# Routing of a fused attention and mixture-of-experts kernel in pieces: batches of 11, 9 and 4 units, four early and six late weight units

## The chip, the cores and the metric

The kernel runs on 1 core of one Trainium2 chip. The metric is the device time of one execution in microseconds (us). The kernel before takes 732.75 us, the median of 3 runs (731.21 to 734.17). Besides these there is one profiled execution, from which all rows below come.

## What is computed

Three layers run one after the other on 3072 tokens of 384 values. Cut to what matters, the reference is:

```python
# 1: gated linear attention, 4 batches x 8 heads x 768 steps, head size 48
state = alpha[t][:, None] * state + outer(k[t], v[t])
x[t] = q[t] @ state
# 2: a router, and 8 experts
do_compute = x @ w_skip > 0
xc = x[do_compute]
e_idx = argmax(xc @ w_gate)
gate_w = softmax(xc @ w_gate)[e_idx]
x[do_compute] = xc + gate_w * (relu(xc @ w1[e_idx]) @ w2[e_idx])   # 384 -> 1024 -> 384
# 3: a dense layer over all tokens
h = x @ w_in                                                       # 384 -> 2048
out = (h - tanh(h)) @ w_out                                        # 2048 -> 384
```

About half of the tokens skip the experts. The weights of the dense layer are float64.

## The kernel before

**Stages.** The order of the instructions on each engine is the order in which the program text issues them. Four stages follow each other.

1. *The attention loop.* `astep(s)` runs for s = 0 to 23. A unit is 128 tokens of one batch entry with all 8 heads, and there are 24. Step s works on several units at once. SP issues the loads `aload(s+4)` (`it`: alpha, q, k) and `vload(s+3)` (`vt`). VectorE runs the two scans of unit s+2 (`F` and `G`, L196 and L203), then the mask of unit s (`am`, L234). GpSimd makes `qh`, `kh` and `pf` of unit s+2 (L209, L214, L221). TensorE makes `pa` of unit s (L229), then `py` of unit s-1 (L243, L250), then `px` of unit s-2 (L297: the token rows and the router's logits), and the state (`pd`, L274, L277). `pa` has one PSUM buffer, so TensorE's `pa` of unit s+1 waits for the mask of unit s. Steps 20 to 23 have no state to update and are shorter.
2. *Fill.* The first `NE0` of the 16 weight units of the dense layer are split into a high and a low part in the attention loop ("early" units, `wsplit`). Row block 0 of the dense layer (512 tokens that skip the experts) is multiplied by these units (`mm1b`, L465, and `mm2b`, L499) while the last routing, the scatters and the first expert weights are under way.
3. *Experts.* 64 weight units, 8 to an expert (`mm1`, L561, and `mm2`, L579 to L581).
4. *Dense layer.* 6 row blocks of 512 tokens by 16 weight units. Block 0 lacks the units that the fill did. The last `NLATE` weight units are split here ("late" units), one every two steps.

**Routing.** Tokens are routed in three batches of units, `BATCHES = (12, 8, 4)`. `route1` (L328 to L352: logits `lg`, maximum `mx`, differences `dl`, the one-hot choice `oa`) and `route1b` (L360 to L369) run on VectorE. `route2` (L376, L378) ranks the tokens of the batch by matmuls of `oa` into `pr` on TensorE, `evr` (L385) copies the ranks to SBUF on ScalarE, and `route3` (L393 to L412) turns them into row numbers `loc` on VectorE. Then `scatter(u)` (L416) writes the 128 rows of unit u to the buffer `xb` in DRAM by an indirect DMA that GpSimd issues. For batch 0, `route1` and `route1b` stand behind the mask in step 13, `route2` at the end of step 13, `evr` and `route3` in step 14; for batch 1 the same in steps 21 and 22. Batch 2 comes behind the loop.

**Around it.** `rload(0)` (L430) reads the 512 rows of block 0 from `xb` on SP in step 21, after all scatters of batch 0. `split2(0, a)` transposes them (L438, TensorE) and splits them in steps 22 and 23. `xload` (L540) reads an expert's rows `xe` from `xb`, and the first two wait for all 24 scatters. The `xb` rows of the experts are first filled from `zero` in steps 6 to 9 (L687). An early weight unit is loaded by `wload` (768 KB, L125) and split in pieces `s0` to `s3`: `s0` (L155, L156), `s1` (L160 and two ScalarE copies), `s2` (L166, L167), `s3` (L170).

The step functions that set the order:

```python
    for k in range(NE0):
        at[max(1, 4 * k)].append(lambda k=k: wload(NMU + k))
        early = wsplit(NMU + k)
        for s, f_ in zip((3, 4, 4, 6), early):
            if k < NE0 - 1:
                aft[4 * k + s].append(f_)
    for i in range(BATCHES[0]):
        aft[14 + 7 * i // BATCHES[0]].append(lambda i=i: scatter(i))
```

`at[s]` runs at the start of step s, and `aft[s]` behind its mask.

Of the kernel before, what the change touches and what calls it, by code (L numbers as in the profile page):

```python
# [21 lines left out]
NU = B * NC_  # L22
# [17 lines left out]
RING = 8  # L40
LA = RING - 3
RAWS = 5
NE0 = 5
NLATE = 5

# [5 lines left out]
TOP = NS + N - 1  # L53
NROWS = NS + N
NCL = NE + 2
BATCHES = (12, 8, 4)
NB = max(BATCHES)
XW = PD + 9

# [2 lines left out]
def tile_kernel(ctx: ExitStack, tc: tile.TileContext, att0, att, vt, wsg, wmoe, wff, out):  # L62
# [56 lines left out]
    def wload(i):  # L119
        if i < NMU or not wide:  # L120
            raw_t[i] = rings["raw"].tile([128, W], F32, tag="raw", name=f"raw{i}")
            nc.sync.dma_start(raw_t[i], wmoe[i] if i < NMU else wff[i - NMU])
        else:
            raw_t[i] = cvp.tile([128, W, 2], U32, tag="raw64", name=f"raw{i}")
            nc.sync.dma_start(raw_t[i].rearrange("p a b -> p (a b)"), wff[i - NMU].bitcast(U32))  # L125

    def wsplit(i):

        own = (ring if i % RING < RING0 else rings["ring2"]) if i < NMU else ffE if i < NMU + NE0 else None
        late = i >= NMU + NF2 - NLATE  # L130
        t_ = {}

        def alloc():
            src = own or rings["late" if late else "R"]
            t_["h"] = src.tile([128, W], F32R, tag="wh", name=f"wh{i}")
            t_["l"] = src.tile([128, W], F32R, tag="wl", name=f"wl{i}")
            w_t[i] = (t_["h"], t_["l"])

        def n0():
            alloc()  # L140
            A.copy(t_["h"], raw_t[i])  # L141

        def n1():
            V.tensor_tensor(t_["l"], raw_t[i], t_["h"].bitcast(F32), ALU.subtract)  # L144

        if i < NMU or not wide:
            return [n0, n1]


        def s0():  # L150
            up = raw_t[i][:, :, 1]
            t_["s"] = cvp.tile([128, W], U32, tag="cs", name=f"cs{i}")
            t_["a"] = cvp.tile([128, W], U32, tag="ca", name=f"ca{i}")
            t_["f"] = cvp.tile([128, W], F32, tag="cl", name=f"cl{i}")
            V.tensor_scalar(t_["s"], up, 3, 0x3FFFFFFF, ALU.logical_shift_left, ALU.bitwise_and)  # L155
            V.scalar_tensor_tensor(t_["a"], up, 0xC0000000, t_["s"], ALU.bitwise_and, ALU.bitwise_or)  # L156

        def s1():
            A.activation(t_["f"], raw_t[i][:, :, 0], AF.Copy, scale=2.0 ** -52)
            V.tensor_scalar(t_["s"], t_["a"], 0xFF800000, None, ALU.bitwise_and)  # L160
            alloc()
            A.copy(t_["h"], t_["a"].bitcast(F32))

        def s2():
            a_ = t_["a"].bitcast(F32)
            V.tensor_tensor(t_["f"], t_["f"], t_["s"].bitcast(F32), ALU.mult)  # L166
            V.tensor_tensor(a_, a_, t_["h"].bitcast(F32), ALU.subtract)  # L167

        def s3():
            V.tensor_tensor(t_["l"], t_["a"].bitcast(F32), t_["f"], ALU.add)  # L170

        return [s0, s1, s2, s3]


    U = [dict() for _ in range(NU)]
# [137 lines left out]
    def t3(n, c, k=NE, dt=F32):  # L313
        return rt.tile([128, NB, k], dt, tag=n, name=f"{n}{c}", bufs=1)[:, :BATCHES[c]]

# [9 lines left out]
    def route1(c):  # L325
        r = RT[c]
        lg = t3("lg", c, 9)
        V.tensor_reduce(lg, r["l4"].rearrange("p b a k -> p b k a"), axis=AX.X, op=ALU.add)  # L328
        mx = t1("mx", c)
        V.tensor_reduce(mx, lg[:, :, 1:9], axis=AX.X, op=ALU.max)  # L330
        dl = t3("dl", c)
        V.tensor_tensor(dl, lg[:, :, 1:9], bc(mx), ALU.subtract)
        r["ex"] = t3("ex", c)
        A.activation(r["ex"], dl, AF.Exp)

        cand = t3("cand", c)
        V.tensor_scalar(cand, dl, 0.0, None, ALU.is_equal)
        V.tensor_tensor(cand, cand, bb(em99, c), ALU.mult)
        fi = t1("fi", c)
        V.tensor_reduce(fi, cand, axis=AX.X, op=ALU.min)  # L340
        V.tensor_scalar(fi, fi, 99.0, None, ALU.add)
        oh = t3("oh", c)
        V.tensor_tensor(oh, bb(eidx, c), bc(fi), ALU.is_equal)

        oa = rt.tile([128, NB + 1, NCL], BF16, tag="oa", name=f"oa{c}", bufs=1)[:, :BATCHES[c] + 1]
        V.memset(oa[:, BATCHES[c]], 0.0)
        r["oaz"], oa = oa, oa[:, :BATCHES[c]]
        ac = t1("ac", c)
        V.tensor_scalar(ac, lg[:, :, 0], 0.0, None, ALU.is_gt)
        V.tensor_tensor(oa[:, :, :NE], oh, bc(ac), ALU.mult)  # L350
        V.tensor_scalar(oa[:, :, NE], ac, -1.0, 1.0, ALU.mult, ALU.add)
        V.tensor_copy(oa[:, :, NE + 1], ac)  # L352
        r["oa"], r["ac"], r["fi"] = oa, ac, fi

    def route1b(c):

# [24 lines left out]
    def evr(c):  # L381
        r = RT[c]
        n = BATCHES[c]
        t_ = rt.tile([128, NB + 1, NCL], F32, tag="prs", name=f"prs{c}", bufs=1)[:, :n + 1]
        A.copy(flat(t_), r["pr"])  # L385
        r["prv"], r["prt"] = t_[:, :n], t_[:, n]
# [27 lines left out]
    def scatter(u):  # L414
        k, i = where[u]
        s_ = nc.gpsimd.indirect_dma_start(  # L416
            xb[:, :], bass.IndirectOffsetOnAxis(loc[:, u:u + 1], 0), RT[k]["xr"][:, i, :], None,
            bounds_check=NROWS - 1, oob_is_err=False)
        if u:
            tc.declare_no_dep(s_.ins, group="route", reason="rows of their own")  # L420
        tc.add_to_no_dep_group("route", s_.ins)
# [263 lines left out]
    for s in range(6, 6 + NS // 512):  # L685
        r0 = 512 * (s - 6)
        at[s].append(lambda r0=r0: nc.sync.dma_start(  # L687
            xb[r0:r0 + 512, :].rearrange("(a p) d -> p a d", a=4), zero.unsqueeze(1).to_broadcast([128, 4, RW])))
    for k in range(NE0):
        at[max(1, 4 * k)].append(lambda k=k: wload(NMU + k))  # L690
        early = wsplit(NMU + k)
        for s, f_ in zip((3, 4, 4, 6), early):
            if k < NE0 - 1:
                aft[4 * k + s].append(f_)
    at[21].append(lambda: rload(0))
    for i in range(BATCHES[0]):
        aft[14 + 7 * i // BATCHES[0]].append(lambda i=i: scatter(i))

    def astep(s):

        def ok(u):
            return 0 <= u < NU

        def pX_(name):
            return ps["T"].tile([128, 512], F32, tag="X", name=name)

        if ok(s + 4):
            aload(s + 4)
        if ok(s + 3):
            vload(s + 3)  # L710
        for f_ in at[s]:
            f_()
        mmA(s)
        if ok(s - 2):
            evx(s - 2)
        c1 = next((k for k in range(len(BATCHES)) if s == first[k] + BATCHES[k] + 1), None)
        c3 = next((k for k in range(len(BATCHES)) if s == first[k] + BATCHES[k] + 2), None)
        if c3 is not None:
            evr(c3)
        if ok(s + 2):  # L720
            scanF(s + 2)
            mkqh(s + 2)
            scanG(s + 2)
            mkkh(s + 2)
            mkpf(s + 2)
        if ok(s - 1):
            mmYs(s - 1)
        trk(s)
        if ok(s - 1):
            evst(s - 1)  # L730
        evk(s)
        if ok(s - 2):
            mmX(s - 2)
            evxa(s - 2)
        mask(s)
        if ok(s - 1):
            mmYa(s - 1)
        if c3 is not None:
            route3(c3)
        if c1 is not None:  # L740
            route1(c1)
            route1b(c1)
        for f_ in aft[s]:
            f_()
        mmS(s)
        if c1 is not None:
            route2(c1, pX_)

    aload(3)
    for s in range(NU - 2):  # L750
# [23 lines left out]
    mmX(NU - 1)  # L774
    evxa(NU - 1)
    early[2]()
    att_ctx.close()
    rings["raw"] = pool("raws", 3, route_ctx, "right")
    part = p0.tile([128, 4, DM], F32, name="part")
# [3 lines left out]
    i0()  # L783
    for i in range(RING0):
        wload(i)
    route1(last)
    fill = [a0()]

    def more(psum):
# [6 lines left out]
    evr(last)  # L796
    route1b(last)
    route3(last)
    early[3]()
    for u in range(first[last], NU):  # L800
        scatter(u)
    psT_ctx.close()
# [5 lines left out]
    for f in range(NE0):  # L808
        if 0 < f < NE0 - 3:
            more(psS)  # L810
        next(fill[f])
        next(fill[f])
        if f + 2 < NE0:
            next(fill[f + 2])
        next(fill[f], None)
        if f == NE0 - 1:
            route_ctx.close()
            rings["ring2"] = pool("ring2", RING - RING0, moe_ctx, "right")
            rings["xe"] = pool("xe", 3, moe_ctx, "right")
            rings["m2"] = pool("m2", 2, moe_ctx, "right")  # L820
            rings["raw"] = pool("raws2", RAWS, moe_ctx, "right")
            xload(0)
            xload(1)
            wload(RING0)
            for a in range(2):
                xprep(0, a)
            for f_ in wsplit(RING0):
                f_()
        mm2b(0, f)
        if f < RING0:  # L830
            for f_ in wsplit(f):
                f_()
    blk0.close()
# [204 lines left out]
```

## Time and profile before

| | |
|---|---|
| median of 3 runs | 732.75 us |
| the profiled execution, its own time | 727.95 us |
| its span, first to last instruction | 726.2 us |
| TensorE matmul busy | 684.0 us (94%) |
| VectorE busy | 441.7 us (61%) |
| ScalarE busy | 301.0 us (41%) |
| GpSimd busy | 146.1 us (20%) |
| TensorE busy in 0 to 150 us | 125.1 of 150 us |
| TensorE busy in 200 to 700 us | 497.6 of 500 us |
| moved by DMA | 81.40 MB, 112 GB/s over the span |

The busy times are of one execution by the hardware profiler. An engine's row tells where it worked, not whether the work set the end. For that one reads what the engine was waiting for: the timeline gives with each instruction the idle time before it and the instruction that ended it. TensorE is nearly always busy behind 200 us, so what it does there moves the end directly; in the first 150 us it waits for others.

### The profile page before, as it was taken

The page shows a single profiled execution, that of the slowest core. Times are in us where ns is not written, and L with a number is a line of the kernel's source. Part 1 is how long each engine was busy: PE and PEld are TensorE (multiplying, and loading weights), DVE is VectorE, ACT ScalarE, POOL GpSimd, SP SyncE. Part 2 cuts the span into 40 slices and gives each one's busy share as a digit, 9 for nine tenths or more (in the row PEclk, how much of TensorE's full clock was granted, in tenths as well). Part 3 has the DMA queues.
Part 4 walks back from the last instruction along what each step waited for, and adds up shares of the span by engine and source line. Part 5 has one row for each costly group of instructions (what it writes and reads, how often), then busy time and mean ns, then how long its engine had stood idle before and what let it go on. Part 6 is the DMA issues. An engine that isn't in the chain of part 4 may idle for free.

```text
span 726.2 us, 11897 instructions
## 1 busy us (share of the span) xinstructions
PE 684.0 (94%) x4707; PEld 629.9 (87%) x4707; DVE 441.7 (61%) x712; ACT 301.0 (41%) x587; POOL 146.1 (20%) x145
## 2 busy tenths in 40 slices
PE   4899799799999999999999999999999999999993
PEld 3799698687999999998988999999989999999892
DVE  8898999876888988948853334333333343343331
ACT  2546455245766656624432333233323332333230
POOL 6655479541011111120011002000200020001002
PEclk9999989999999999999999999999999999999997
DMA  9979959345779778613110001001100110001001
GB/s 276 205 198 284 230 133 243 99 154 182 262 250 327 265 245 262 206 32 129 45 56 32 1 22 67 0 1 45 45 0 1 46 43 1 1 5 39 1 1 47
DMA packets 30543, 81.40 MB, mean 112 GB/s; under 512 B 4405, under 2 KB 14677, under 8 KB 30480
## 3 DMA queue, kind: packets, MB, share of 16 engines
q1 hardware_dynamic: 26384, 68.64, 32.5%
q0 software_dynamic: 4096, 11.92, 4.6%
q8 instruction: 39, 0.64, 0.4%
q14 instruction: 24, 0.20, 0.1%
HBM read 65.45 MB, written 15.84 MB: 112 GB/s over the span
## 4 chain that ended last, share of the span: by engine, by line
issue 53%; PE 26%; DVE 11%; DMA 4%; POOL 3%; ACT 2%; SPq 0%; POOLq 0%; DVEq 0%; ACTq 0%
PE hp L561 8%; DMA it<-in_att_dram 4%; PE yp L579 3%; PE yp L580 3%; PE yp L581 3%; DVE F L196 2%; POOL out_dram L513 2%; PE pa L229 2%; PE py L243 2%; PE px L297 1%; DVE G L203 1%; DVE am L234 1%; PE py L250 1%; DVE wl L144 1%; DVE ca L167 1%
## 5 line engine op out<-in xcount | busy, mean ns | idle before, releaser
L473 DVE TENSOR_TENSOR g<-h,g 128x512 f32<-128x512 f32 x96 | 66.3, 690 | 156.0 <-ACT g L471 156.0
L499 PE MATMUL y<-wh,gl 128*128 128x384 f32 x384 | 130.2, 339 | 0.3
L499 PE MATMUL y<-wh,gh 128*128 128x384 f32 x384 | 129.9, 338 | 0.7 <-ACT gh L475 0.7
L499 PE MATMUL y<-wl,gh 128*128 128x384 f32 x384 | 129.6, 338 | 0.0
L471 ACT ACTIVATE g<-h 128x512 f32<-128x512 f32 x96 | 57.2, 597 | 165.3 <-PE h L465 165.3
L465 PE MATMUL h<-xh,wh 128*128 128x512 f32 x288 | 115.2, 400 | 1.2 <-DVE g L473 1.2
L465 PE MATMUL h<-xh,wl 128*128 128x512 f32 x288 | 113.5, 394 | 0.4 <-DVE wl L170 0.4
L465 PE MATMUL h<-xl,wh 128*128 128x512 f32 x288 | 113.6, 394 | 0.0
L477 DVE TENSOR_TENSOR gl<-g,gh 128x512 fp32r<-128x512 f32 x96 | 66.4, 692 | 60.6 <-ACT gh L475 42.1
L475 ACT CAST gh<-g 128x512 fp32r<-128x512 f32 x96 | 59.6, 621 | 91.7 <-DVE g L473 91.7
L513 POOL DMA_INDIRECT out_dram<-ob,id x24 | 23.6, 983 | 366.4 <-DVE ob L512 308.0
L499 PEld LDWEIGHTS y<-wh,gh 128*128 128x128 f32 x384 | 72.1, 188 | 5.6 <-ACT gh L475 1.7
L499 PEld LDWEIGHTS y<-wl,gh 128*128 128x128 f32 x384 | 72.2, 188 | 4.1
L499 PEld LDWEIGHTS y<-wh,gl 128*128 128x128 f32 x384 | 72.1, 188 | 1.8 <-DVE gl L477 1.8
L465 PEld LDWEIGHTS h<-xl,wh 128*128 128x128 f32 x288 | 54.0, 188 | 12.5
L141 ACT CAST wh<-raw 128x768 fp32r<-128x768 f32 x64 | 53.4, 835 | 24.3 <-PE yp L581 22.3
L465 PEld LDWEIGHTS h<-xh,wh 128*128 128x128 f32 x288 | 54.1, 188 | 10.4 <-DVE g L473 1.6
L144 DVE TENSOR_TENSOR wl<-raw,wh 128x768 fp32r<-128x768 f32 x64 | 60.7, 949 | 2.8 <-ACT wh L141 2.8
L465 PEld LDWEIGHTS h<-xh,wl 128*128 128x128 f32 x288 | 54.2, 188 | 9.2 <-DVE wl L170 0.7
L561 PE MATMUL hp<-eh,wh 128*128 128x256 f32 x192 | 55.8, 290 | 1.3 <-DVE hl L566 1.3
L561 PE MATMUL hp<-eh,wl 128*128 128x256 f32 x192 | 53.8, 280 | 0.0
L561 PE MATMUL hp<-el,wh 128*128 128x256 f32 x192 | 53.7, 280 | 0.0
(141 smaller groups left out, 1157.6 us busy)
## 6 DMA issues: line engine op xcount, KB each, us to landing
raw<-in_wmoe_dram SPq DMA_DIRECT2D x64, 384.0 KB, 4.0
raw<-in_wff_dram SPq DMA_DIRECT2D x16, 768.0 KB, 5.0
it<-in_att_dram SPq DMA_DIRECT2D x40, 289.5 KB, 8.4
rows<-xb SPq DMA_DIRECT2D x6, 776.0 KB, 4.4
vt<-in_vt_dram SPq DMA_DIRECT2D x24, 192.0 KB, 5.8
xb<-zero SPq DMA_DIRECT2D x4, 776.0 KB, 7.1
xe<-xb SPq DMA_DIRECT2D x8, 388.0 KB, 4.6
it<-in_att_dram SPq DMA_DIRECT2D x2, 772.0 KB, 8.1
```

Source lines behind the costliest of these rows:

```text
L141: A.copy(t_["h"], raw_t[i])
L144: V.tensor_tensor(t_["l"], raw_t[i], t_["h"].bitcast(F32), ALU.subtract)
L465: T.matmul(hp, *todo.pop(0), start=len(todo) == last, stop=not todo)
L471: A.activation(g, hp, AF.Tanh)
L473: V.tensor_tensor(g, hp, g, ALU.subtract)
L475: A.copy(gh, g)
L477: V.tensor_tensor(gl, g, gh.bitcast(F32), ALU.subtract)
L499: T.matmul(o, g_[:, sl_], w_[:, DM:], start=first and n == 0, stop=last and n == len(todo) - 1)
L513: s_ = nc.gpsimd.indirect_dma_start(out[:, :], bass.IndirectOffsetOnAxis(d["id"][:, a:a + 1], 0), ob, None, bounds_check=N - 1, oob_is_err ...
L561: T.matmul(hp, w_[:, ks], x_[:, k], start=n == 0, stop=n == 3 * KT - 1)
L579: T.matmul(o, hh[:, sl_], wh[:, DM:], start=f == 0, stop=False)
L580: T.matmul(o, hh[:, sl_], wl[:, DM:], start=False, stop=False)
```

## The change

The sizes change: batches of 11, 9 and 4 units, 4 early weight units, 6 late ones. `route1` becomes a generator with two pieces. Its pieces, `route1b` and `route3` are called from `aft`, one in a step: for batch 0 in steps 12, 13, 14 and 15, for batch 1 in steps 21, 22 and both last in 23. `route2` and `evr` stand together near the start of step 14 (23 for batch 1), behind `mmA` and `evx`. The early units are loaded in steps 1, 6, 12 and 19, and their split has five pieces (`s2` in two). The scatters of batch 0 go into steps 15 to 20, one and then two in a step.

```diff
-NE0 = 5
-NLATE = 5
+NE0 = 4
+NLATE = 6
...
-BATCHES = (12, 8, 4)
+BATCHES = (11, 9, 4)
...
-    def wsplit(i):
+    def wsplit(i, fine=False):
...
+        def s2a():
+            V.tensor_tensor(t_["f"], t_["f"], t_["s"].bitcast(F32), ALU.mult)
+
+        def s2b():
+            a_ = t_["a"].bitcast(F32)
+            V.tensor_tensor(a_, a_, t_["h"].bitcast(F32), ALU.subtract)
+
         def s2():
-            a_ = t_["a"].bitcast(F32)
-            V.tensor_tensor(t_["f"], t_["f"], t_["s"].bitcast(F32), ALU.mult)
-            V.tensor_tensor(a_, a_, t_["h"].bitcast(F32), ALU.subtract)
+            s2a()
+            s2b()
...
-        return [s0, s1, s2, s3]
+        return [s0, s1, s2a, s2b, s3] if fine else [s0, s1, s2, s3]
...
         V.tensor_reduce(mx, lg[:, :, 1:9], axis=AX.X, op=ALU.max)
+        yield
         dl = t3("dl", c)
...
         r["oa"], r["ac"], r["fi"] = oa, ac, fi
+        yield
...
-    for k in range(NE0):
-        at[max(1, 4 * k)].append(lambda k=k: wload(NMU + k))
-        early = wsplit(NMU + k)
-        for s, f_ in zip((3, 4, 4, 6), early):
-            if k < NE0 - 1:
-                aft[4 * k + s].append(f_)
+
+    for k, (ld, s0) in enumerate(((1, 4), (6, 8), (12, 16), (19, 0))):
+        at[ld].append(lambda k=k: wload(NMU + k))
+        early = wsplit(NMU + k, fine=True)
+        if s0:
+            for s, f_ in zip((0, 1, 1, 2, 3), early):
+                aft[s0 + s].append(f_)
+    route = [route1(c) for c in range(len(BATCHES))]
+
+    def advance(c):
+        next(route[c])
+
+    def rank(c, psum):
+        route2(c, psum)
+        evr(c)
+
+    ranks = {first[1] + 3: 0, NU - 1: 1}
+    for s, c, f_ in ((first[1] + 1, 0, advance), (first[1] + 2, 0, advance), (first[1] + 3, 0, route1b),
+                     (first[1] + 4, 0, route3),
+                     (NU - 3, 1, advance), (NU - 2, 1, advance), (NU - 1, 1, route1b), (NU - 1, 1, route3)):
+        aft[s].append(lambda c=c, f_=f_: f_(c))
+    for i in range(BATCHES[0]):
+        aft[15 + (i + 1) // 2].append(lambda i=i: scatter(i))
     at[21].append(lambda: rload(0))
-    for i in range(BATCHES[0]):
-        aft[14 + 7 * i // BATCHES[0]].append(lambda i=i: scatter(i))
...
-        c1 = next((k for k in range(len(BATCHES)) if s == first[k] + BATCHES[k] + 1), None)
-        c3 = next((k for k in range(len(BATCHES)) if s == first[k] + BATCHES[k] + 2), None)
-        if c3 is not None:
-            evr(c3)
+        if s in ranks:
+            rank(ranks[s], pX_)
...
-        if c3 is not None:
-            route3(c3)
-        if c1 is not None:
-            route1(c1)
-            route1b(c1)
         for f_ in aft[s]:
             f_()
         mmS(s)
-        if c1 is not None:
-            route2(c1, pX_)
...
     early[2]()
+    early[3]()
...
-    route1(last)
+    advance(last)
+    advance(last)
...
-    early[3]()
+    early[4]()
...
         if f == NE0 - 1:
+            for f_ in wsplit(f):
+                f_()
             route_ctx.close()
...
-        if f < RING0:
+        if f < NE0 - 1:
             for f_ in wsplit(f):
                 f_()
```

Three places show what it does to the order of an engine. The lines of the changed program lie 6 to 18 further down.

TensorE around the ranking of batch 0, before: `pd` is the end of step 13, `pr` the ranking, `pa` the start of step 14.

```order
L250 MATMUL py_125<-am_1041,vt_782 48x128 x8
L277 MATMUL pd<-vt_851,kt_1107 64x48 x8
L376 LDWEIGHTS tri
L376 MATMUL pr_1169<-oa_1142,tri 128x130
...
L378 MATMUL pr_1169<-oa_1142,ones 128x10
L229 MATMUL pa_1187<-qh_1011,kh_1015 128x128 x8
L243 MATMUL py_126<-qh_936,st_120 128x128 x4
```

The same place in the changed kernel:

```order
L256 MATMUL py_125<-am_1034,vt_773 48x128 x8
L283 MATMUL pd<-vt_848,kt_1097 64x48 x8
L235 MATMUL pa_1151<-qh_1004,kh_1008 128x128 x8
L384 LDWEIGHTS tri
L384 MATMUL pr_1162<-oa_1130,tri 128x120
...
L386 MATMUL pr_1162<-oa_1130,ones 128x10
L249 MATMUL py_126<-qh_933,st_120 128x128 x4
```

The ranking moved behind the first matmuls of step 14.

VectorE around `route1` of batch 0, before: `F`, `G` and `am` are the scans and the mask, all routing of batch 0 up to `xr` stands between a mask and the next scan.

```order
L234 TENSOR_TENSOR am_1116<-pa_1072,maskT 128x1024
L328 TENSOR_REDUCE lg_1126<-l_329 128x108
L330 TENSOR_REDUCE mx_1128<-lg_1126 128x12
L332 TENSOR_TENSOR dl_1130<-lg_1126,mx_1128 128x96
...
L352 CAST oa_1142<-ac_1144 128x12
L360 CAST sel_1149<-oa_1142 128x12
...
L369 TENSOR_TENSOR xr_328<-ev_1156,fi_1137 128x12
L196 SCALAR_TENSOR_TENSOR F_1200<-it_95,ind 128x512
```

The same in the changed kernel, from the mask of step 12 on:

```order
L240 TENSOR_TENSOR am_1034<-pa_990,maskT 128x1024
L334 TENSOR_REDUCE lg_1044<-l_329 128x99
L336 TENSOR_REDUCE mx_1046<-lg_1044 128x11
L202 SCALAR_TENSOR_TENSOR F_1073<-it_98,ind 128x512
...
L240 TENSOR_TENSOR am_1108<-pa_1062,maskT 128x1024
L339 TENSOR_TENSOR dl_1118<-lg_1044,mx_1046 128x88
...
L359 CAST oa_1130<-ac_1132 128x11
L202 SCALAR_TENSOR_TENSOR F_1177<-it_95,ind 128x512
```

Scans and a mask now stand between the pieces, and `oa` is made one step ahead of its use.

GpSimd at the end of the attention loop, before (`xb<-xr` is the scatter; 328, 1231 and 1820 are batches 0, 1 and 2):

```order
L416 DMA xb<-xr_328,loc 5120x388 x2
L209 TENSOR_TENSOR qh_1674<-it_97,F_1671 128x512
L214 TENSOR_TENSOR kh_1678<-it_97,G_1676 128x512
L416 DMA xb<-xr_328,loc 5120x388
L209 TENSOR_TENSOR qh_1724<-it_98,F_1721 128x512
L214 TENSOR_TENSOR kh_1728<-it_98,G_1726 128x512
L416 DMA xb<-xr_1231,loc 5120x388 x8
```

and in the changed kernel (328 and 1104 are batches 0 and 1):

```order
L424 DMA xb<-xr_328,loc 5120x388 x2
L215 TENSOR_TENSOR qh_1652<-it_97,F_1649 128x512
L220 TENSOR_TENSOR kh_1656<-it_97,G_1654 128x512
L424 DMA xb<-xr_328,loc 5120x388 x2
L215 TENSOR_TENSOR qh_1705<-it_98,F_1702 128x512
L220 TENSOR_TENSOR kh_1709<-it_98,G_1707 128x512
L424 DMA xb<-xr_1104,loc 5120x388 x9
```

Step 20 holds two scatters where it held one, and nine follow the last `kh` where there were eight.

## Rows read from the trace of the kernel before

**Rows 1.** The page's slices of the span: TensorE's busy tenths.

```profile
PE   4899799799999999999999999999999999999993
```

**Rows 2.** Timeline of TensorE, steps 5 and 13 to 15: start, duration, instruction, idle before.

```profile
35.98 1.16 PE L229 MATMUL pa<-qh,kh 64*128 64x128 f32 x16 [3.04 <-DVE am L234]
...
81.30 1.16 PE L229 MATMUL pa<-qh,kh 64*128 64x128 f32 x16 [0.52 <-DVE am L234]
...
91.00 0.27 PE L376 MATMUL pr<-oa,tri 128*128 128x130 bf16 x1 [4.35 <-DVE oa L352]
...
91.86 2.08 PE L229 MATMUL pa<-qh,kh 64*128 64x128 f32 x16
...
98.88 1.16 PE L229 MATMUL pa<-qh,kh 64*128 64x128 f32 x16
```

**Rows 3.** Windows: busy us of TensorE, its loads, VectorE, ScalarE, GpSimd; granted clock, DMA.

```profile
92.00:95.40 3.40, 3.40 (x23) 3.17 (x24) 3.33 (x4) 0.86 (x3) 1.94 (x2) 0.50 0.04 13
...
37.10:40.60 3.50, 3.50 (x21) 3.50 (x19) 3.43 (x5) 1.89 (x5) 0.89 (x1) 0.57 1.00 245
```

**Rows 4.** Timeline of TensorE, the starts of steps 18, 20 and 23 and batch 1's ranking.

```profile
116.08 1.16 PE L229 MATMUL pa<-qh,kh 64*128 64x128 f32 x16 [1.31 <-DVE am L234]
...
126.64 1.16 PE L229 MATMUL pa<-qh,kh 64*128 64x128 f32 x16
...
139.37 0.20 PE L376 MATMUL pr<-oa,tri 128*128 128x90 bf16 x1 [4.37 <-DVE oa L352]
...
146.17 1.16 PE L229 MATMUL pa<-qh,kh 64*128 64x128 f32 x16
```

**Rows 5.** Timeline of VectorE: routing of batch 0, then a scan and a mask.

```profile
87.48 0.90 DVE L328 TENSOR_REDUCE lg<-l 128x108 f32<-128x432 f32 x1
...
88.70 0.26 DVE L332 TENSOR_TENSOR dl<-lg,mx 128x96 f32<-128x96 f32 x1
...
90.81 0.18 DVE L360 CAST sel<-oa 128x12 f32<-128x12 bf16 x1
...
91.85 1.22 DVE L196 TENSOR_TENSOR_SCAN F<-it,ind 128x512 f32<-128x512 f32 x1
...
95.58 0.55 DVE L393 TENSOR_TENSOR rk<-prs,cnt 128x120 f32<-128x120 f32 x1
...
97.94 0.95 DVE L170 TENSOR_TENSOR wl<-ca,cl 128x768 fp32r<-128x768 f32 x1
...
130.63 3.12 DVE L196 TENSOR_TENSOR_SCAN F<-it,ind 128x512 f32<-128x512 f32 x1
...
135.22 1.20 DVE L234 TENSOR_TENSOR am<-pa,maskT 128x1024 f32<-128x1024 f32 x1
```

**Rows 6.** Timeline of GpSimd: a product, the last scatters of batches 0 and 2.

```profile
131.40 1.27 POOL L214 TENSOR_TENSOR kh<-it,G 128x512 f32<-128x512 f32 x1
132.83 1.74 POOL L416 DMA_INDIRECT xb<-xr,loc  x1 [0.17 <-issue]
...
166.64 0.97 POOL L416 DMA_INDIRECT xb<-xr,loc  x1 [0.30 <-issue]
```

**Rows 7.** Issues on SP's queue; then the DMA engines' busy tenths, 136 to 141 us.

```profile
136.40 0.38 SPq L430 DMA_DIRECT2D rows<-xb  x1
...
170.26 0.89 SPq L540 DMA_DIRECT2D xe<-xb  x2
...
DMA  0000000000039994577999999999999951005000
```

**Rows 8.** Timeline of TensorE: the first matmul of the fill and of the experts.

```profile
155.56 0.48 PE L465 MATMUL h<-xh,wh 128*128 128x512 f32 x1
...
180.26 0.28 PE L561 MATMUL hp<-eh,wh 128*128 128x256 f32 x1
```

**Rows 9.** Timeline of TensorE, dense layer: first matmuls of two neighbouring units.

```profile
381.09 0.39 PE L465 MATMUL h<-xh,wh 128*128 128x512 f32 x1
...
385.27 0.39 PE L465 MATMUL h<-xh,wh 128*128 128x512 f32 x1
```

## The prediction

> **What bounds the kernel now.** I read the page's slices first. TensorE is full from the ninth slice on and has gaps in the first eight, 0 to 145 us [rows 1]: behind 200 us a change pays only by moving TensorE's own work, ahead of it by removing what TensorE waits for. So I went to TensorE's timeline, where each row names what ended the idle time before it. An undisturbed step of the attention loop lasts 5.28 us: steps 18 and 19 run from 116.08 to 126.64, which is 10.56 [rows 4]. Two places stand out. Ahead of the ranking of batch 0 TensorE waits 4.35 us for `oa` on VectorE [rows 2], and ahead of that of batch 1 4.37 us [rows 4]. Then VectorE's timeline: in that time it does the routing, one instruction behind the other [rows 5]. Last the windows, for the granted clock: it is 0.50 of full, the lower level (1.2 GHz), for 3.4 us behind the first of these waits [rows 3].
>
> **The change, part by part.** I count how much earlier the kernel reaches three points: step 23, the experts, the end.
>
> *Batch 0.* Step 13 starts at 81.30 and step 14 at 91.86 [rows 2], 10.56 us for a step of 5.28. Of the excess, 91.00 to 91.86 is the ranking itself (0.86), which stays, so 5.28 - 0.86 = 4.42 goes. Step 14 lasts to 98.88, 7.02 us, 1.74 over 5.28: the low clock [rows 2, 3]. Without the wait that goes too. Gain 4.42 + 1.74 = 6.2.
>
> *Batch 1.* The mask of step 21 ends at 135.22 + 1.20 = 136.42 [rows 5]; step 22 now needs only this, where the ranking began at 139.37 [rows 4]: 2.95. The ranking leaves step 22 (0.35, an estimate: nine small matmuls for the 13 of 0.86, each shorter). The low clock goes again; I take 1.6, a little under the 1.74 of batch 0, as step 22 has fewer matmuls. Gain 2.95 + 0.35 + 1.6 = 4.9. Both together 11.1.
>
> *VectorE in the loop.* The work is not gone, it is spread. Two scans and a mask take 95.58 - 91.85 = 3.73 of each step [rows 5]. The routing pieces are 88.70 - 87.48 = 1.22, 90.81 - 88.70 = 2.11, 91.85 - 90.81 = 1.04 and 97.94 - 95.58 = 2.36 [rows 5], in steps 12 to 15. The split of the third early unit is six instructions of about 0.95 (as `wl` in [rows 5]) in steps 16 to 19. Steps 12 to 19 hold 8 x 3.73 + 6.7 + 5.7 = 42.2 us of VectorE against 8 x 5.28 + 0.86 = 43.1 of TensorE. That just fits, if nothing is stretched. But a scan of 1.22 us took 3.12 [rows 5] when `kh` ran on GpSimd from 131.40 to 132.67 [rows 6], 1.9 more. Walking the steps through, I find VectorE about 0.4 us late with `oa` in step 14 and with masks 0.6 and 0.9 late in steps 18 and 19, in place of the 1.31 us wait of [rows 4], and about 1 us late in steps 20 and 21, which are short. Net I take -1.4. The ends: +1.3 (the old wait goes, none comes) and -3.8 (two more collisions of 1.9). Gain at step 23: 9.7.
>
> *Why scan and product collide* is told by the Trainium skill, page "SBUF — State Buffer", section "Who interferes with whom": a VectorE instruction with two SBUF inputs and a GpSimd instruction that reads SBUF take a shared port in turn, each for its whole length. That speaks against this change, which puts the two-input instructions of routing and split between GpSimd's products. Our scan, stretched to the end of `kh` and about 1 us beyond, agrees. With free overlap instead, the 1.4 above would be no loss and the forecast 1.4 us lower; with the rule at its hardest the third rival holds, at its price.
>
> *The rows of block 0.* Here a wait takes the place of one removed. `rload(0)` waits for the last scatter of batch 0. That one started at 132.83 [rows 6], the load was issued at 136.40, and the DMA engines were done with it 34 slices of 0.125 us behind 136, at 140.2 [rows 7]: 7.4 us from scatter to rows. In step 22 TensorE wanted them about 0.8 us ahead of step 23 [rows 4], at 145.4, and had 5 us to spare. Step 20 started at 126.64 [rows 4], so the last scatter came 6.2 behind it. Now step 20 holds a second scatter (1.74 + 0.17, [rows 6]) and GpSimd comes to it with some 0.9 us of backlog from two scatters in every step from 16 on: 9.0, and rows at 9.0 + 7.4 = 16.4 behind step 20. TensorE wants them at 19.5 - 4.9 + 1.0 - 0.8 = 14.8. It waits 1.6. The ends are 0 (no backlog, and step 20 as late as VectorE makes it) and 3.5 (one more collision). Gain at step 23: 9.7 - 1.6 = 8.1.
>
> *From step 23 to the experts.* Before, this took 180.26 - 146.17 = 34.1 us [rows 4, 8]: 9.4 to the fill, then five units in 24.7, 4.94 each. With four units TensorE alone could be there at 9.4 + 1.4 + 4 x 4.94 = 30.6, where 1.4 is the ranking of batch 1 and what `route1b` and `route3` (1.04 + 2.36, less when nine units wide) delay the last copy on VectorE. But the rows of the experts are later. Nine scatters start only behind `route3` of step 23, by my walk 6.6 us into it, and the four of batch 2 queue behind them on GpSimd. A scatter takes 0.97 + 0.30 [rows 6], so the last starts at 6.6 + 12 x 1.27 = 21.8; before it was 166.64 - 146.17 = 20.5. The load of `xe` follows 170.26 - 166.64 = 3.6 behind [rows 6, 7], and from there the experts began 10.0 later, with TensorE busy in between; landing, transposes, split and the last unit's second half need about 7. That makes 21.8 + 3.6 + 7 = 32.4, so 1.7 of the 4.9 us is gained. Ends: 0 and 3.5. Gain at the experts: 9.8.
>
> *The moved unit.* The fifth early unit becomes a late one and takes a full step of the dense layer: 385.27 - 381.09 = 4.18 us [rows 9]. Its split has VectorE's spare time there. -4.2.
>
> *The loads* of the early units (step 6 for 4, 12 for 8, one less in all) I cost at nothing. The wait of 3.04 in step 5 [rows 2] stands ahead of them. The load that comes among the `zero` fills in step 6 replaces the one of step 8, and by step 13, which waited 0.52 [rows 2], as much has been moved as before. If that cover fails, a scan is late by some 1 us; if it does better, the 0.52 goes. The experts' and late units' loads keep their order.
>
> *The sum.* 11.1 - 1.4 - 1.6 + 1.7 - 4.2 = 5.6 us. Against the profiled execution's own 727.95 that is 722.3. The median of the runs lies 4.8 above that execution, so I forecast **732.75 - 5.6 = 727.2**.
>
> **The rivals.**
>
> 1. *VectorE keeps up and the rows are in time.* For it: 42.2 against 43.1. Against: the stretched scan. Both losses go: 5.6 + 1.4 + 1.6 = 8.6, or 724.2.
> 2. *The wait for the rows costs the clock.* In step 5 a wait of 3.04 us [rows 2] was followed by a clock of 0.57 [rows 3]; the wait of 1.31 was not, since the two steps behind it took 5.28 each [rows 4]. If the rows are 3.5 us late the clock falls too: 5.6 - 1.9 - 1.7 = 2.0, or 730.8: no change that can be told.
> 3. *The scatters become the bound, and it is slower.* One takes 1.74 + 0.17 us beside VectorE's scans and 0.97 + 0.30 without them [rows 6], 0.64 apart. If the collisions stretch all ten that stand in steps 16 to 20, ahead of the rows, and the nine of step 23, ahead of the experts' rows, that is 19 x 0.64 = 12.2 us on the two chains for which TensorE waits: 5.6 - 12.2 = -6.6, or 739.4. It decides from 0.3 us a scatter on (19 x 0.3 = 5.7). For it: VectorE has less idle time now. Against: the short scatter is the last one of batch 2, beside routing and splitting too, and GpSimd has a step of lead with `kh`.
> 4. *The pieces do not take the wait away.* VectorE is 2 to 3 us late with `oa`, as the scan ahead of it waits for its load: 5.6 - 2.3 = 3.3, or 729.5.
>
> **How the numbers follow.** A measurement of this kernel tells about 0.5% from no change, 3.7 us. The forecast has 0.48 (its own range 725.2 to 729.2), the rivals 0.17, 0.22, 0.08 and 0.05. Faster: 0.41 of the forecast and rival 1, 0.58. Same: the rest of the forecast, and rivals 2 and 4, nearly all, 0.33. Slower: rival 3 and a tail of 2, 0.09. The range reaches a little past rivals 1 and 2, to 723.6 and 732.4, and leaves out rival 3 and the far ends of the bounds.
>
> **What would show it.** In the profile after: no idle time over 1 us ahead of `pr` of batches 0 and 1, and clock 1.00 behind it; step 15 starting near 93; waits under 1 us for the mask in steps 18 to 21; a wait of about 1.6 us ahead of the first transpose of step 22, and none for its rows under rival 1; the experts' first matmul near 170.5; a dense layer 4.2 us longer. It is wrong if step 23 starts later than 141 (rivals 2 and 3) or the experts wait for `xe` by several us.

## The result, and the profile after

The kernel before took 733.46 us (median of 4 runs, 731.21 to 734.71), the changed one 726.00 us (4 runs, 724.22 to 726.64): ratio 0.9894, 95% interval 0.9868 to 0.9919. It is 7.5 us faster, where 5.6 were forecast. The profiled execution of the changed kernel took 726.17 us (span 724.5), as its other runs do. That of the kernel before had taken 727.95, and none of its later runs on the first three chips took less than 731.06. This turned out to matter, so the kernel before was profiled once more, in an execution of 733.58 us (span 731.9). Starts in us:

| reached | before [rows 2, 4, 8] | before, again | after |
|---|---|---|---|
| step 13 | 81.30 | 78.22 | 76.12 |
| step 15 | 98.88 | 95.23 | 87.75 |
| step 20 | 126.64 | 123.58 | 115.71 |
| step 23 | 146.17 | 144.32 | 133.20 |
| experts | 180.26 | 186.04 | 169.84 |
| end of span | 726.2 | 731.9 | 724.5 |

The page's slices of the changed kernel, TensorE's busy tenths and its clock, against [rows 1]:

```profile
PE   4999998868999999999999999999999999999993
...
PEclk9999999989999999999999999999999999999997
```

The fifth and the eighth slice, 7 before, are 9 and 8. The deepest is now the ninth, 145 to 163 us, and it is the only one ahead of the last whose digit of the clock is under 9. Now TensorE's timeline, against [rows 2, 4]:

```profile
33.41 1.16 PE L235 MATMUL pa<-qh,kh 64*128 64x128 f32 x16 [0.57 <-DVE am L240]
...
76.12 1.16 PE L235 MATMUL pa<-qh,kh 64*128 64x128 f32 x16
...
83.16 0.21 PE L384 MATMUL pr<-oa,tri 128*128 128x120 bf16 x1 [0.60 <-DVE oa L359]
...
87.75 1.16 PE L235 MATMUL pa<-qh,kh 64*128 64x128 f32 x16
...
110.20 1.16 PE L235 MATMUL pa<-qh,kh 64*128 64x128 f32 x16 [0.85 <-DVE am L240]
...
121.32 1.16 PE L235 MATMUL pa<-qh,kh 64*128 64x128 f32 x16 [1.47 <-DVE am L240]
...
132.39 0.87 PE L446 MATMUL px<-ident,rows 128*128 128x128 f32 x6 [2.28 <-DMA rows<-xb]
```

The wait of 4.35 us for `oa` is 0.60, that of batch 1 is gone. Small waits for masks stand ahead of steps 18 to 22, 3.36 us in all, and one of 2.28 us for the rows ahead of step 23. The windows show what the clock did behind them (busy us of TensorE, its loads, VectorE, ScalarE, GpSimd; clock, DMA), against [rows 3]:

```profile
82.00:86.00 4.00, 3.40 (x45) 3.13 (x43) 3.85 (x11) 1.94 (x6) 1.52 (x2) 1.00 1.04 188
...
133.20:137.00 3.80, 3.80 (x51) 3.58 (x52) 3.43 (x5) 1.75 (x6) 0.00 (x0) 1.00 0.00 0
...
150.00:156.00 6.00, 0.04 (x1) 0.04 (x1) 2.54 (x14) 1.19 (x3) 1.51 (x3) 0.69 0.17 66
156.00:159.50 3.50, 3.50 (x9) 2.77 (x10) 2.29 (x4) 1.84 (x3) 2.69 (x3) 0.55 0.30 114
...
175.50:181.00 5.50, 5.50 (x28) 5.50 (x29) 3.36 (x6) 3.30 (x6) 0.00 (x0) 0.69 1.01 385
```

The clock held at 1.00 (2.4 GHz) behind the short waits. It fell behind two waits that nobody had forecast. The first, in the timelines of TensorE, ScalarE and VectorE:

```profile
147.20 0.24 PE L386 MATMUL pr<-oa,ones 128*128 128x40 bf16 x4
...
155.96 0.79 PE L473 MATMUL h<-xh,wl 128*128 128x512 f32 x1 [6.10 <-DVE wl L176]
...
153.13 0.20 ACT L393 COPY prs<-pr 128x50 f32<-128x50 f32 x1 [8.14 <-remote]
...
153.36 0.20 DVE L401 TENSOR_TENSOR rk<-prs,cnt 128x40 f32<-128x40 f32 x1 [6.08 <-ACT prs L393]
...
154.95 0.95 DVE L176 TENSOR_TENSOR wl<-ca,cl 128x768 fp32r<-128x768 f32 x1
```

Read it backwards, from TensorE: it waits for `wl` of the fourth early unit, which stands on VectorE behind the ranking of batch 2, which waits for `prs`, and ScalarE copies `prs` 5.7 us after the last `pr` matmul (147.44). For this wait the profile names no instruction that ended it (`remote`). The trace has TensorE's semaphore raised at 153.05, 0.1 us ahead of the copy, so it was not ScalarE that was late. The ends of matmuls are modelled in a profile: whether these ended late or only told of it late, it can't say. The nine scatters of batch 1 run beside this, from 139.97 to 151.34. The second wait, at the experts' start:

```profile
172.34 0.83 ACT L141 CAST wh<-raw 128x768 fp32r<-128x768 f32 x1 [2.55 <-DMA raw<-in_wmoe_dram]
...
174.55 0.40 ACT L573 ACTIVATE hh<-hp 128x256 fp32r<-128x256 f32 x1
...
175.48 0.39 PE L569 MATMUL hp<-eh,wh 128*128 128x256 f32 x1 [2.80 <-DVE hl L574]
```

ScalarE waits for the weights of unit 4, with the first `hh` queued behind.

### The profile page after: what moved, and what is told of

The parts are those of the page before. It is cut to its first block, busy times and chain, and to the rows that moved or that the text cites. A ratio compares the mean times of both kernels' runs of the same rounds, so it can differ in the third digit from the quotient of the medians.

```text
span 724.5 us, 11897 instructions
## 1 busy us (share of the span) xinstructions
PE 681.0 (94%) x4707; PEld 627.1 (87%) x4707; DVE 439.4 (61%) x712; ACT 301.0 (42%) x587; POOL 144.1 (20%) x145
## 4 chain that ended last, share of the span: by engine, by line
issue 52%; PE 17%; DVE 3%; POOL 2%; DMA 1%; ACT 0%; POOLq 0%; SPq 0%; ACTq 0%
PE hp L569 8%; PE yp L587 3%; PE yp L588 3%; PE yp L589 3%; POOL out_dram L521 2%; DVE wl L144 1%; PE pe L446 1%; DMA raw<-in_wmoe_dram 0%; DVE xe L596 0%; DVE ca L156 0%; DVE hl L574 0%; DVE ca L169 0%; DVE cl L165 0%; DVE el L449 0%; DVE cs L155 0%
```

## The experiments

Each is an edit of the changed kernel, if nothing else is said; its label stands in brackets. Times are medians, ratios are to the kernel before, which ran beside each set. The first set (after_again, load4, whole, wl_first), the second (before_again, split_later, scat_late, five_early) and the third (hold9, hold5, scat_early) ran on a chip each, where the kernel before took 733.9 to 734.2 us; hold3 ran on a fourth. A trace is of one execution, which need not lie at the median; where it lies far from it, that is said.

**The kernel before again** (before_again).

> The kernel before, unedited, with a new profile. Its first profiled execution (727.95 us) lay 3 us under the fastest of its 20 other runs (731.06). If TensorE's signals reach the other engines late beside the scatters in this kernel too, as they do in every profile of the changed kernel, a run near 733 shows it: prs of batch 2 some us behind its last matmul, and the experts starting later than 34.1 us behind step 23. If not, the difference lies in the early steps: waits of 3 us and more for the masks of steps 5 to 9.

Timelines of TensorE and ScalarE in step 23 and behind it, then windows:

```profile
146.41 1.14 PE L297 MATMUL px<-selw,xT 128*128 128x105 f32 x8
...
151.91 0.46 PE L250 MATMUL py<-am,vt 128*48 128x128 f32 x4 [0.73 <-issue]
153.32 1.54 PE L250 MATMUL py<-am,vt 128*48 128x128 f32 x12 [0.96 <-issue]
...
151.92 0.19 ACT L305 COPY l<-px 128x36 f32<-128x36 f32 x1 [5.57 <-PE py L243]
```

```profile
155.00:159.00 4.00, 2.60 (x12) 2.60 (x13) 2.90 (x5) 1.87 (x5) 0.00 (x0) 0.50 0.76 282
159.00:163.00 4.00, 4.00 (x14) 3.32 (x14) 2.33 (x16) 0.84 (x4) 0.00 (x0) 0.50 0.00 1
```

The copy of `l` came 4.4 us behind its matmuls, which ended at 147.55 (`px` on L297); TensorE itself stood still three times for nothing that the profile shows, and the clock was 0.50 for 8 us behind it. Batch 1's eight scatters ran until 152.2. Step 23 to the experts took 41.7 us, where the first profile has 34.1. `prs` of batch 2, ranked long after the scatters here, was on time: the lateness is there, in another place than I expected.

**The changed kernel again** (after_again).

> The changed kernel a second time, unedited. If the late end of the ranking of batch 2 (its copy prs on ScalarE started 5.7 us behind its last matmul) belongs to this program, the gap of about 6 us ahead of the fourth early unit's second matmul comes again near 156 us; if it was a chance of one execution, it is missing here and the experts start about 5 us earlier. Time 724 to 727 either way.

725.84 us, ratio 0.9897 (0.9869 to 0.9926). The late `prs` came again: last `pr` matmul 145.26, copy 150.89, TensorE idle for 6.04. So did the second wait, 3.13. The wait of step 5 was 0.57 in the one execution and none in the other: it is no fixed cost.

**Routing in one piece** (whole). The order of the kernel before comes back for the routing and for the scatters of batch 0:

```
-        aft[s].append(lambda c=c, f_=f_: f_(c))
...
-        aft[15 + (i + 1) // 2].append(lambda i=i: scatter(i))
+        aft[14 + 7 * i // BATCHES[0]].append(lambda i=i: scatter(i))
...
-        if s in ranks:
-            rank(ranks[s], pX_)
...
+            advance(c1)
+            advance(c1)
+            route1b(c1)
...
+            route2(c1, pX_)
```

> The routing of batches 0 and 1 is in one piece again, as in the kernel before, with the scatters of batch 0 where they stood; the early units' loads, four early and six late units and batches of 11, 9 and 4 stay. Theory 1 (the waits for oa cost what the prediction took, 11.1 us, of which 1.4 and 1.6 were given back): two waits of about 4 us ahead of the rankings with a clock near 0.5 behind them, step 23 starting some 8 us later than in the changed kernel, near 141, and a time of 732 to 735. Theory 2 (behind step 23 the late ranking of batch 2 and the rows of the experts set the pace, and half of this is hidden there): 728 to 731.

734.36 us, ratio 1.0007 (0.9987 to 1.0027): all of the gain is gone, 8.5 us against the changed kernel, and the time is near the upper end of theory 1. Its TensorE timeline has the two waits back, against [rows 2, 4]:

```profile
84.70 0.26 PE L384 MATMUL pr<-oa,tri 128*128 128x120 bf16 x1 [3.95 <-DVE oa L359]
...
136.89 0.24 PE L384 MATMUL pr<-oa,tri 128*128 128x100 bf16 x1 [3.44 <-DVE oa L359]
```

So the pieces, with the places of the ranking and of batch 0's scatters that go with them, are worth 8.5 us, and the rest of the change (loads, four and six units, batch sizes) nothing, taken together. The trace is of the slowest of the 13 runs, 741.20 us. In it steps 12 to 22 took 69.3 us (75.40 to 144.74) against 62.4 in the changed kernel (70.84 to 133.20), so 7.0 of the 8.5 can be seen where the argument has them. Step 23 started at 144.74 and not near 141: it was 4.6 late at step 12 already, of which a wait of 3.53 in step 5.

**The second load back in step 4** (load4).

```
-    for k, (ld, s0) in enumerate(((1, 4), (6, 8), (12, 16), (19, 0))):
+    for k, (ld, s0) in enumerate(((1, 4), (4, 8), (12, 16), (19, 0))):
```

> The second early unit is loaded in step 4 again, as in the kernel before, and all else is the changed kernel. Theory 1 (the place of this load gave the 5 us by which the changed kernel was ahead at step 13): the wait of about 3 us and the low clock come back in step 5, step 13 starts near 81 in place of 76, and the time is 3 to 5 us over the changed kernel's, about 729 to 731. Theory 2 (the 5 us came from lighter loads in general, a unit less in all): step 13 still starts near 76 to 77, and the time is within 1 us of the changed kernel's 726.

728.83 us, ratio 0.9930 (0.9907 to 0.9954): 3.0 us slower than the changed kernel, the low end of theory 1, but not by the wait in step 5, which was none. It is step 8 that waited, 2.43 us, and with slow matmuls it then took 6.86 in place of 5.28:

```profile
51.67 2.08 PE L235 MATMUL pa<-qh,kh 64*128 64x128 f32 x16 [2.43 <-DVE am L240]
58.53 1.16 PE L235 MATMUL pa<-qh,kh 64*128 64x128 f32 x16
```

Why a load in step 4 makes step 8 wait was not tried.

**Five early units, with the pieces** (five_early).

```
-NE0 = 4
-NLATE = 6
+NE0 = 5
+NLATE = 5
...
+    for k, (ld, s0) in enumerate(((1, 4), (6, 8), (9, 12), (12, 16), (19, 0))):
...
```

> Five early units and five late ones again, with the routing in pieces: a load in step 9, a fourth split in steps 12 to 15. Theory 1 (the prediction's term: a unit moved to the dense layer costs 4.2 us there, and the fill ahead of the experts waits for the rows anyway, so the fifth unit is mostly covered): about 3 us gained, 722 to 724. Theory 2 (VectorE has no room for six more instructions of about 1 us in steps 12 to 15, and every collision with GpSimd's products makes TensorE wait): steps 12 to 16 are 4 to 6 us longer, with the low clock behind a wait, and the time is 727 to 731.

730.08 us, ratio 0.9954 (0.9939 to 0.9970), in the range of theory 2: 4.2 us slower than the changed kernel, though the dense layer has a unit less. TensorE waits in steps 13 and 14 and for `oa`:

```profile
77.39 1.16 PE L235 MATMUL pa<-qh,kh 64*128 64x128 f32 x16 [1.74 <-DVE am L240]
83.89 1.16 PE L235 MATMUL pa<-qh,kh 64*128 64x128 f32 x16 [1.15 <-DVE am L240]
87.69 0.21 PE L384 MATMUL pr<-oa,tri 128*128 128x120 bf16 x1 [2.64 <-DVE oa L359]
```

Steps 12 to 14 took 23.6 us here (70.30 to 93.91) and 16.9 in the changed kernel (70.84 to 87.75): with this unit's split left in the loop, VectorE has no room for the pieces. The size of the loss is not explained by this, though. The trace is of the fastest of six runs, 725.02 us, where the other five took 729.25 to 732.60. It reaches the experts 7.6 us later than the changed kernel's trace and wins 8.7 back behind them. What the other runs lost besides, no trace shows.

**The late signal: wl first, and scatters held back** (wl_first, scat_late, hold9). The first edit moves `early[4]()` up to `early[3]()`, ahead of the routing of batch 2.

> The last piece of the fourth early unit's split (wl) stands ahead of the routing of batch 2 on VectorE, no longer behind it. Theory 1 (TensorE waits 6.1 us only because wl is queued behind a ranking that waits for prs): the gap before the fourth unit's second matmul goes, but the next one, for gh of the first unit, is still bound by prs near 153, so 1 to 2 us are gained: 724 to 725. Theory 2 (prs comes late because TensorE stands still): prs comes at about 148, and 4 to 6 us are gained: 720 to 722.

725.36 us, ratio 0.9886 (0.9860 to 0.9913). The wait for `wl` went, but others came in its place: 1.67 us that the profile explains by nothing and 3.38 for `gh`. `prs` was 2.7 us late (147.54 to 150.24), half of what it was, for no reason found. No gain that can be told, nearest to theory 1. The second edit writes the nine scatters of batch 1 behind the routing of batch 2:

> The nine scatters of batch 1 stand behind the routing of batch 2 instead of ahead of it, so that no scatter runs while batch 2 is ranked. Theory 1 (TensorE's signals are late because of the scatters running beside them): prs starts within 0.1 us of the last pr matmul, near 147.5 by the times of the changed kernel's profile. Theory 2 (the late signal has another cause, such as the loads or code): prs still comes 3 to 6 us late. The time is no aim here: the rows of the experts come some 3 us later and TensorE waits for them, 726 to 730.

725.04 us, ratio 0.9894 (0.9872 to 0.9916). This told nothing: GpSimd had no work ahead of these scatters, so they started at 138.0 all the same, and `prs` was 4.8 us late (in a trace of the fastest of its four runs, 721.29). To hold them back really, GpSimd has to wait for `prs`:

```
-    aft[NU - 1].append(lambda: [scatter(u) for u in range(first[1], first[last])])
...
+    dep = cp.tile([128, 1], F32, name="dep")
+    G.tensor_tensor(dep, RT[last]["prt"][:, :1], RT[last]["prt"][:, :1], ALU.mult)
+    for u in range(first[1], first[last]):
+        scatter(u)
```

> The changed kernel, but GpSimd makes one tiny product that reads prs of batch 2 before the nine scatters of batch 1, so now they really can't run while batch 2 is ranked (in the run called scat_late they had only been written later, and GpSimd, which had nothing ahead of them, ran them at the same time as before). Theory 1 (TensorE's signals come late because of a close series of scatters beside them): prs starts within 0.1 us of the last pr matmul, and the late signals move to the matmuls behind it, beside the thirteen scatters that now run in one series. Theory 2 (another cause): prs still comes 4 to 6 us late. Thirteen scatters of 1.28 us from about 146 end near 163, xe is asked for near 166 in place of 161 to 163, and the time is 728 to 732.

727.43 us, ratio 0.9927 (0.9899 to 0.9955). ScalarE, GpSimd and TensorE:

```profile
145.60 0.20 ACT L393 COPY prs<-pr 128x50 f32<-128x50 f32 x1 [2.74 <-PE pr L386]
...
146.68 1.01 POOL L424 DMA_INDIRECT xb<-xr,loc  x1 [0.59 <-DVE bs L409]
...
169.96 1.30 PE L446 MATMUL pe<-ident,xe 128*128 128x128 f32 x5 [10.62 <-DMA xe<-xb]
```

`prs` came 0.1 us behind its matmul (145.51): without the scatters beside it, the signal is on time. But the second half of theory 1 fell: the thirteen scatters ran in one series up to 164.7, beside the fill's matmuls, and none of their signals was late. A series alone is not enough, then. The price is the wait of 10.62 us for `xe`.

**Splits two steps later** (split_later).

```
-            for f_ in wsplit(RING0):
-                f_()
...
+    for k, f_ in zip((1, 2), wsplit(RING0)):
+        at[k].append(f_)
...
-        s_ = j - LA
+        s_ = j - LA + 2
```

> The splits of the experts' weight units from the fifth on stand two steps later in the experts' stage, so that ScalarE no longer waits for raw of unit 4 ahead of the first hh. Theory 1 (the 2.8 us gap and the low clock behind it at the experts' start come from that wait on ScalarE): the gap goes and the clock stays at 1.00, 3 to 4.5 us gained, 721.5 to 723. Theory 2 (the weights' transfers themselves are the bound, with the DMA queues full there): the gap moves to the first matmul of unit 4, 0 to 1 us gained, 725 to 726.

721.36 us, ratio 0.9833 (0.9812 to 0.9855): theory 1, some 4.5 us better than the changed kernel, which ran on another chip (ratio 0.9897). In the timeline of ScalarE `hh` is ahead, and the window behind it has the full clock:

```profile
169.81 0.38 ACT L573 ACTIVATE hh<-hp 128x256 fp32r<-128x256 f32 x1 [0.82 <-PE hp L569]
170.39 0.83 ACT L141 CAST wh<-raw 128x768 fp32r<-128x768 f32 x1 [0.19 <-DMA raw<-in_wmoe_dram]
```

```profile
173.00:179.00 6.00, 6.00 (x46) 5.96 (x45) 3.54 (x7) 3.13 (x7) 0.00 (x0) 1.00 0.98 384
```

**On top of that kernel** (hold5, scat_early), first five of batch 1's scatters held back as above:

> The kernel with the splits two steps later (721.4 us), and the last five of batch 1's nine scatters held back behind prs in the same way. Theory 1 (late signals go with a close series of scatters): four scatters are over by 143.5 and landed by 146, prs comes at most 1 us late, and the other nine end near 158 as before, so the experts start up to 2 us earlier: 719.5 to 721.5; if signals of the fill's matmuls now come late beside the nine, nothing is gained: 721 to 723. Theory 2 (another cause): prs is as late as before and the held scatters come 5 us later: 725 to 728.

722.01 us, ratio 0.9836 (0.9812 to 0.9859): no gain. `prs` was on time (147.62 to 147.72), but TensorE then waited 4.81 us for `xe`. Late signals and late rows came to about the same here.

Then the scatters of batch 0 (`15 + i // 2` for `15 + (i + 1) // 2`):

> The kernel with the splits two steps later (721.4 us), and the scatters of batch 0 spread as two in each of steps 15 to 19 and one in step 20, where it was one in step 15 and two in step 20. Theory 1 (the last scatter of batch 0 sets when the rows of block 0 come, as the prediction had it): it starts about 1.9 us earlier, the wait of about 1.5 us ahead of the first transpose of step 22 goes, 1 to 1.5 us are gained: 720 to 720.5. Theory 2 (the gain is lost in the wait for the scatters of batch 1, which is bound by GpSimd and not by step 23's start alone, or VectorE is stretched in step 15): 0 to 0.5 us gained, 721 to 722.

721.25 us, ratio 0.9822 (0.9804 to 0.9840): theory 2. GpSimd, SP's queue and TensorE of this kernel, and then of the one without the edit, whose steps 20 started at 118.02 and 114.84 us:

```profile
124.50 1.75 POOL L424 DMA_INDIRECT xb<-xr,loc  x1 [0.17 <-issue]
...
128.90 0.38 SPq L438 DMA_DIRECT2D rows<-xb  x1
...
133.37 0.88 PE L446 MATMUL px<-ident,rows 128*128 128x128 f32 x6 [1.00 <-DMA rows<-xb]
```

```profile
123.39 0.97 POOL L424 DMA_INDIRECT xb<-xr,loc  x1 [0.30 <-issue]
...
126.41 0.38 SPq L438 DMA_DIRECT2D rows<-xb  x1
...
130.75 0.87 PE L446 MATMUL px<-ident,rows 128*128 128x128 f32 x6 [1.55 <-DMA rows<-xb]
```

The last scatter starts 6.5 us behind step 20 in place of 8.6, but it now runs beside a scan and takes 1.75 us, not 0.97, and the load behind it is asked for only 0.7 earlier (10.9 for 11.6).

**Three edits together** (hold3).

> Three edits together, as a candidate for the fastest: the splits two steps later, two scatters of batch 0 in each of steps 15 to 19 with one in step 20, and only the last three of batch 1's nine scatters held back behind prs. Theory 1 (prs is late as long as a series of scatters stands ahead of it, and the experts then wait for the last scatter): six scatters are over when batch 2 is ranked, prs comes at most 1 us late, the last scatter starts some 3 us earlier after step 23 than with five held, the stretch from step 23 to the experts is about 35 us in place of 36.5, and the time is 719.5 to 720.5. Theory 2 (six scatters are enough for late signals): prs is 2 to 5 us late again, the held scatters come later still, and the time is 721 to 724.

717.02 us, on a chip where the kernel before took 726.54 (724.97 to 727.86): ratio 0.9866 (0.9850 to 0.9883). `prs` was on time (151.40 to 151.49), the experts waited 1.90 us for `xe`, and step 23 to the experts took 32.8, in a trace of the slowest of its five runs (720.46). It beats the kernel before. The time is below theory 1's, but that was stated for chips where the kernel before takes 734. By the ratio it is no better than split_later (0.9833) or scat_early (0.9822), whose kernels before were 7 us slower on their chips. So neither theory is confirmed, and which of these kernels is the fastest stays open.

## Why the prediction was right, point by point

The time lay where it was forecast, 1.2 us off, and the reason given for the gain is shown: without the pieces nothing is left of it. But outside the heart of the loop the sum did not hold: the loads, the way from step 23 to the experts, the experts' stage and the frame came out otherwise, and their errors largely cancel. By the stretches of the table, against the first profile and then against the second:

- *Steps 13 to 23, the heart of the argument.* The steps forecast 11.1 - 1.4 - 1.6 = 8.1 us. Found: (146.17 - 81.30) - (133.20 - 76.12) = 7.8, and 9.0 against the second profile. Batch 0 alone: from step 13 to 15 17.58 became 11.63, so 5.95 for the 6.2 less 0.4. The collisions and the rows cost more than forecast: 0.60 ahead of `pr` and waits for masks of 3.36 in place of the old 1.31, which is 2.65 for 1.4, and 2.28 for 1.6 (1.47 in the repeat). That the sum held all the same is due to batch 1, whose gain I had too small: without these waits steps 20 to 22 took 13.2 us for 19.5 before, 6.3 for 4.9. Of the signs named, one missed: the mask wait ahead of step 21 was 1.47, over the 1 us. The clock stayed up behind all of them, so the second rival did not come. The first fell by the waits that are there, the fourth by 0.60 ahead of `pr`. The third fell too: step 23 came 13 us earlier.
- *The loads, which the sum took at nothing.* Step 13 came 5.2 us earlier, and 2.1 against the second profile. Putting one load back cost 3.0 us, so by the medians this term is about +3. The ranges of the runs overlap (723.89 to 729.18 and 726.72 to 729.85), and the traces alone don't show it: nine with the load in step 6 reach step 13 at 75.22 to 80.38 us, load4 at 79.64. The cover I named, the wait in step 5, is not fixed to the load. It was 0 to 3.65 us long with the load in step 6.
- *Step 23 to the experts, +1.7.* Against the first profile it was -2.6 (34.1 to 36.6), against the second +5.1. My walk had the scatters as the bound, at 32.4, ahead of TensorE's own 30.6, and took signals to be on time. What failed is that `prs` came 5.7 us late. The scatters of batch 2 started at 155.52, 22.3 us behind step 23, where I had their last one at 21.8. Yet TensorE did not wait for `xe` in this trace: the late `prs` reached it by `wl`, on a path that my walk did not have, as a wait of 6.10 us with the clock at 0.55 behind it.
- *The moved unit, -4.2.* The dense layer, from its first matmul to the end of the span, took 403.2 us before (from 323.00) and 407.4 after (from 317.10): 4.1. That step was right. In the experts' stage ahead of it, for which the sum had no term, 4.5 us were lost (142.7 to 147.3), by the split of unit 4. I had written that the experts' loads keep their order. They do, but the pool for the load of unit 4 opens behind the last split of units 0 to 3, and with an early unit less that split stands right ahead of it: the load was issued at 176.37, 3.9 us ahead of the experts' first matmul, and is now issued at 168.92, 0.9 ahead. Putting the splits two steps later gave the 4.5 us back: the stage then took 141.9.
- *The frame.* I took the 4.8 us between the profiled execution and the median for a constant of both kernels. In the second profile of the kernel before, 5.7 us longer, it is the stretch behind step 23 that is longer, by 7.6 us, with the late signals in it, and the change alters these. Between the two first profiles, one without late signals and one with them, the gain is 1.8 us only; between the two with them it is 7.4. That the total held is luck in these terms; that the loop held, in its cause and about in its size, is not.

The lines behind the last points are the first matmul of the dense layer and SP's issue of unit 4's load, each before and then after:

```profile
323.00 0.40 PE L465 MATMUL h<-xh,wh 128*128 128x512 f32 x1
...
176.37 5.48 SPq L122 DMA_DIRECT2D raw<-in_wmoe_dram  x6
```

```profile
317.10 0.40 PE L473 MATMUL h<-xh,wh 128*128 128x512 f32 x1
...
168.92 5.60 SPq L122 DMA_DIRECT2D raw<-in_wmoe_dram  x6
```

Collisions between VectorE and GpSimd stand in the changed kernel's timelines, here `cs` of the third early unit beside `kh`. It has one input. The same instruction of the fourth unit, with no product of GpSimd beside it, took 0.55 us at 140.36:

```profile
103.77 1.49 DVE L160 TENSOR_SCALAR cs<-ca 128x768 uint32<-128x768 uint32 x1
...
103.55 1.28 POOL L220 TENSOR_TENSOR kh<-it,G 128x512 f32<-128x512 f32 x1
```

The Trainium skill, page "SBUF — State Buffer", section "Who interferes with whom", says that such a one-input instruction can contend with GpSimd as well, in its two-port form; the 1.49 agrees. Which form it ran in, no trace shows.

Open: what makes TensorE's signals late. The changed kernel was not run on the fourth chip, where the kernel before took 726.54, near its first profile, so whether the chips differ in this, and how much the change gains there, was not tried.

## What to carry to other kernels

Cut serial work of an engine in pieces only as far as its idle time goes: with the pieces and a unit's split taken out of the loop the kernel was 7.5 us faster than before, with the pieces and that split left in about half of that. When a stage gets shorter, look at once at what its end opens (a pool, a load, a queue behind it), since that moves towards its user. And profile the kernel before twice before a profile stands for a median.

## What was not expected of the hardware

Beside the scatters of batch 1, TensorE's matmuls were known to ScalarE late: 5.5 to 5.7 us behind their modelled end in both profiles of the changed kernel and in load4, split_later and scat_early, 2.7 to 4.8 us in wl_first, five_early and scat_late, 4.4 us in the second profile of the kernel before and 7.3 us in whole (its `px` ended at 148.40, the copy of `l` started at 155.68). In the five with 5.5 to 5.7 the copy came 0.4 to 0.6 us behind the end of the last packet of batch 1's scatters. With the scatters held back it was 0.1 us in three profiles (hold9, hold5, hold3). Yet in the first profile of the kernel before eight scatters ran in such a series, and in hold9 thirteen, with every signal in time. Loads of weights beside them are not what it takes: in the second profile of the kernel before and in whole none ran in the late stretch. A load of instructions, one packet of 8 KB, stands in or just ahead of the late stretch in every late profile (at 146.66 in the changed kernel's first), but also beside the scatters in the first profile of the kernel before (148.92), where nothing was late. What else it takes was not found.
